# Two-level Strassen in the first MLP layer of the last two pairs

## The chip, the cores and the metric

The kernel runs on one core of one Trainium2 chip. Its engines each have their own instruction stream, in a fixed order: PE (TensorE: matmuls, with their weight loads shown as PEld), DVE (VectorE), ACT (ScalarE), POOL (GpSimd) and SP (SyncE, which here only issues DMAs). They wait for each other by semaphores. SBUF is the working memory of 128 partitions; PSUM, into which PE writes, has 8 banks of 512 fp32 per partition. The metric is the device time in microseconds, the median of several executions.

## The reference

```python
# attention: q, k, v [4, 8, 768, 64], blocks of 64 with a decaying state
for b in range(nb):
    intra = np.einsum('bhic,bhjc->bhij', qb, kb) * Dmask[None]
    intra = np.einsum('bhij,bhjd->bhid', intra, vb)
    inter = np.einsum('bhid,bhde->bhie', qb * lam_pow[None], kv_state)
    out[:, :, sl] = intra + inter
    kv_state = lam_block[None, :, None, None] * kv_state + np.einsum('bhsd,bhse->bhde', kb_dec, vb)
# then, with x [4, 768, 512] the heads side by side:
mixed = np.real(np.fft.fft(np.fft.fft(x, axis=1), axis=2))
u = x + mixed
un = (u - mu) / np.sqrt(var + 1e-06)          # over the last axis
ch = np.maximum(un @ w_ch1, 0.0) @ w_ch2      # 512 -> 2048 -> 512
out = u + ch
```

All of it is fp32. The change concerns `relu(un @ w_ch1)` for a third of the rows.

## The kernel before, in words

The 3072 rows are handled in 12 groups of 256 rows (two tiles of 128). The front (attention, Fourier mixing, normalisation) runs for all; the first four groups go through the MLP in the plain way while the fronts of later batches still run. The other eight groups, `LATE`, write their normalised rows transposed to DRAM (`utd`), and their rows `u` too (`ud`), and are done at the end, two groups at a time: four **pairs**, numbered 0 to 3, in `late(j)`. From about 439 us on there is only this work.

A pair computes both layers as one Strassen-Winograd product each: seven half-size products in place of eight, listed in `PRODUCTS` as (combination of weights or hidden rows, combination of the other operand). For the first layer the weights' combinations (`s2.A`) are made once; a pair's input combinations t1 to t4 are four sums on DVE (L737 to L740).

*First layer before.* For each of eight hidden chunks `i` of 128, the seven products are two accumulating matmuls of 128x128 by 256 columns each (`prod`, L773). Each fp32 matmul is two PE instructions, so this is 7*2*8*2 = 224 instructions per pair. ACT and DVE take the results out of PSUM in pieces of 256 elements per partition, apply the relu and form the sums that the second layer wants.

*Second layer.* It is Strassen a second time inside each of the seven products (`level2`): 49 quarter products of four 128x128 by 128 matmuls, so 49*4*2 = 392 instructions (L890). Within a product the seven quarter products come in groups 0 to 6 of eight PE instructions, and use three PSUM banks: X takes groups 0, 2, 4 and 6 one upon the other, Y group 1, Z groups 3 and 5. After each group the bank is read, by ACT where the target is fresh, else by an adding DVE operation:

```python
prod(X, S2, T2, False)
give(X, 1, 0, True)
```

As X goes on accumulating, group 2 can only be written when the read of group 0 is done, and so on. Two products are therefore interleaved by the loop at the end of `late`: product k gives its groups at the steps 7k, 7k+2, ..., 7k+12, so that in the steady state every step holds one group, and what follows a product is put down at step 7k+14. There are 8 bank buffers (`p2`), taken in turn.

The inner sums of the weights of the second layer (`td`) are made by POOL during pair 0's first layer (`keep_sums`: four sums per product, 28 in all, of 512 elements per partition), stored in DRAM, and loaded again by each pair, three tiles of 256 KB per product, into the six `tx` buffers. The inner sums of the hidden rows are made by DVE (`prepare_a`), in `sx` buffers, one product ahead. `split` replaces a quarter of an operand by a difference in place.

*Order.* Operations are recorded in the order of the Python code, and a scheduler of the framework then fixes an order per engine; what is pinned with `keep_in_program_order` stays. Each engine works strictly through its order, and an instruction whose semaphore is late holds all behind it. DMAs issued on SP's and ACT's queues (`nc.sync`, `nc.scalar`) wait in the same way. After product 4 of the second layer, DVE and POOL add the rows `u` (L843 on POOL, L870 on DVE) and the rows of the pair are stored (`store`: an SP DMA for one tile of each group, a POOL indirect DMA for the other).

Of the kernel before, what the change touches and what calls it, by code (L numbers as in the profile page):

```python
# [76 lines left out]
def kernel(  # L77
# [647 lines left out]

    def load_u(j, queue=nc.sync):

        r = s2.u[j] = new(s2.up, [128, 2, KO, G * 128], "ur")
        for h, (b, g) in enumerate(LATE[2 * j:2 * j + 2]):
            queue.dma_start(r[:, h], utd[b, g])  # L730


    def late(j):
        r = s2.u.pop(j)
        b11, b21, b12, b22 = r[:, 0, 0:2], r[:, 0, 2:4], r[:, 1, 0:2], r[:, 1, 2:4]
        t1, t2, t4 = (new(s2.hp, [128, 2, G * 128], "sx", bufs=7) for _ in range(3))
        V.tensor_tensor(t1, b12, b11, op=SUB)  # L737
        V.tensor_tensor(t2, b22, t1, op=SUB)  # L738
        V.tensor_tensor(t4, b21, t2, op=SUB)
        V.tensor_tensor(b12, b22, b12, op=SUB)  # L740
        U = dict(b11=b11, b21=b21, b22=b22, t1=t1, t2=t2, t4=t4, t3=b12)

        h = {n: new(s2.hp, [128, G, HF, 128], f"h{n}") for n in ("a11", "a12", "a22", "s1", "s3")}

        pre_a, pre_b = {}, {}

        def split(t):

            A11, _, A21, _ = quarters_a(t)
            tc.keep_in_program_order(V.tensor_tensor(A21, A11, A21, op=SUB))  # L750

        def prepare_a(k):

            a = PRODUCTS[k][0]
            A11, A12, A3, A22 = quarters_a(h[a])
            S1, S2, S4 = pre_a[k] = [new(s2.hp, [128, HF // 2, 128], "sx", bufs=7) for _ in range(3)]
            V.tensor_tensor(S2, A22, A3, op=SUB)
            yield 0.0
            V.tensor_tensor(S1, S2, A11, op=ADD)
            yield 0.0  # L760
            V.tensor_tensor(S4, A12, S2, op=SUB)
            yield 0.0

        def prepare_b(k):

            pre_b[k] = [new(s2.yp, [128, HF // 2, HM // 2], "tx", bufs=6) for _ in range(3)]
            for i in (1, 0, 2):
                nc.sync.dma_start(pre_b[k][i], s2.td[k][i])
                yield 0.0
# [9 lines left out]
        def bank():  # L779
            return new(s2.ps, [128, DM], "p2")[:, 0:G * 128]  # L780

        def finish(i, X, Z):
            a11, a12, a22, s1, s3 = (h[n][:, :, i, :] for n in ("a11", "a12", "a22", "s1", "s3"))
            prod(X, "s4", "b22", i, False)
            a21 = new(s2.hp, [128, G, 128], "a21", bufs=2)
# [7 lines left out]
        who = [[(b, TT[g][s]) for s in range(G)] for b, g in LATE[2 * j:2 * j + 2]]  # L793
        us = [new(s2.yp, [128, G, DM], "u2", bufs=2) for _ in range(2)]

        def load_x():
            for k in range(2):
                for s in range(G):
                    tc.keep_in_program_order(nc.sync.dma_start(us[k][:, s], ud[who[k][s]]))

        last = None
        for i in range(HF):
            a11, a12, a22 = (h[n][:, :, i, :] for n in ("a11", "a12", "a22"))
            X, Y, Z = bank(), bank(), bank()
# [15 lines left out]
            if j == 0 and i < len(PRODUCTS):  # L820
                if i == 0:
                    tc.keep_in_program_order(nc.gpsimd.tensor_copy(s2.begun, h["a11"][:, 0, 0, 0:1]))
                keep_sums(i)
            if i == HF - 3:
                load_x()
            if i == HF - 2:
                for k in range(2):
                    run(prepare_b(k))
            if i > HF // 2:
                split(h[("a11", "a12", "s3")[i - HF // 2 - 1]])  # L830
        run(prepare_a(0))
        finish(*last)
        run(prepare_a(1))
        if 2 * j + 2 < len(LATE):
            load_u(j + 1)

        yt = new(s2.yp, [128, 2, G, DM], "y2")
        T = new(s2.yp, [128, G, HM], "t2")
        y11, y12, y21, y22 = (yt[:, k, :, m:m + HM] for k in range(2) for m in (0, HM))

        def add_u(k, m, y):
            u = us[k][:, :, 0:HM] if m == 0 else us[k][:, :, DM - 1:HM - 1:-1]
            nc.gpsimd.tensor_tensor(y, y, u, op=ADD)  # L843

        def part_sum(o, x, y, op):

            for s in range(G):
                V.tensor_tensor(o[:, s], x[:, s], y[:, s], op=op)

        def after(k):  # L850

            if k == 0:
                h["s2"] = h["a11"]
                split(h["s1"])
                part_sum(h["a11"], h["s1"], h["a11"], SUB)
            elif k == 1:
                V.tensor_tensor(y11, y11, T, op=ADD)  # L857
                add_u(0, 0, y11)
            elif k == 2:
                split(h["a22"])  # L860
                h["s4"] = h["a12"]
                part_sum(h["a12"], h["a12"], h["s2"], SUB)
            elif k == 3:
                V.tensor_tensor(y21, T, y22, op=ADD)
                add_u(1, 0, y21)
            elif k == 4:
                V.tensor_tensor(y12, y12, T, op=ADD)
                V.tensor_tensor(y22, y22, y12, op=ADD)
                add_u(1, 1, y22)
                V.tensor_tensor(y12, y12, us[0][:, :, DM - 1:HM - 1:-1], op=ADD)  # L870
            elif k == 5:
                store(*who[1][1], yt[:, 1, 1])
            else:
                store(*who[0][1], yt[:, 0, 1])
                store(*who[1][0], yt[:, 1, 0])
                store(*who[0][0], yt[:, 0, 0])

        outs = [(T, True), (y11, True), (y22, True), (T, False), (y12, True), (y21, False), (y12, False)]

        def level2(k):  # L880

            (a, b), (y, fresh) = PRODUCTS[k], outs[k]
            A11, A12, A3, A22 = quarters_a(h[a])
            B11, T3, B21, B22 = quarters_b(s2.B[b])
            (S1, S2, S4), (T1, T2, T4) = pre_a.pop(k), pre_b.pop(k)
            X, Y, Z = (bank()[:, 0:HM // 2] for _ in range(3))

            def prod(ps, a, b, first):
                for i in range(HF // 2):
                    nc.tensor.matmul(ps, lhsT=a[:, i, :], rhs=b[:, i, :], start=(first and i == 0),  # L890
                                     stop=(i == HF // 2 - 1), skip_group_check=True)

            def give(ps, s, m, first=False):
                o = y[:, s, m * HM // 2:(m + 1) * HM // 2]
                if first and fresh:
                    nc.scalar.copy(o, ps)  # L896
                else:
                    V.tensor_tensor(o, ps, o, op=ADD)  # L898

            prod(X, A11, B11, True)  # L900
            give(X, 0, 0, True)
            yield 0.0
            prod(Y, A12, B21, True)
            give(Y, 0, 0)
            yield 0.0
            prod(X, S2, T2, False)
            give(X, 1, 0, True)
            yield 0.0
            prod(Z, A3, T3, True)
            give(Z, 1, 1, True)  # L910
            yield 0.0
            prod(X, S1, T1, False)
            give(X, 1, 1)
            yield 0.0
            prod(Z, A22, T4, False)
            give(Z, 1, 0)
            yield 0.0
# [101 lines left out]
    for j in range(len(LATE) // 2):  # L1019
        late(j)  # L1020
# [30 lines left out]
```

## Time and profile before

| | |
|---|---|
| median of 3 runs (lowest, highest) | 812.43 us (809.25, 812.84) |
| profiled execution, its own time | 816.68 us |
| its span, first to last instruction | 814.9 us |
| granted TensorE clock | 0.993 |
| PE busy | 780.8 us, 5280 instructions |
| DVE, ACT, POOL busy | 545.7, 203.6, 142.2 us |
| L773 on the chain, first layer of the pairs | 24% |
| L890 on the chain, second layer of the pairs | 19% |

A group of instructions in the profile is named by line, engine, operation, and output<-input by tile names, where `p` is a PSUM bank of the late stage, `ur` the loaded inputs, `w` and `w1s` the weights and their sums, `ha` and `hs` the hidden rows (a11, a12, a22; s1, s3), `sx` and `tx` the inner sums, `y` the output rows. Behind `x` stands the count, then busy time and the mean of one in ns, then the idle time ahead of them and what ended it. Matmuls overlap, so their mean (379 ns at L773, 275 at L890) is longer than their spacing, which the chain of work shows.

### The profile page before, as it was taken

The page shows a single profiled execution, that of the slowest core. Times are in us where ns is not written, and L with a number is a line of the kernel's source. Part 1 is how long each engine was busy: PE and PEld are TensorE (multiplying, and loading weights), DVE is VectorE, ACT ScalarE, POOL GpSimd, SP SyncE. Part 2 cuts the span into 40 slices and gives each one's busy share as a digit, 9 for nine tenths or more (in the row PEclk, how much of TensorE's full clock was granted, in tenths as well). Part 3 has the DMA queues.
Part 4 walks back from the last instruction along what each step waited for, and adds up shares of the span by engine and source line. Part 5 has one row for each costly group of instructions (what it writes and reads, how often), then busy time and mean ns, then how long its engine had stood idle before and what let it go on. Part 6 is the DMA issues. An engine that isn't in the chain of part 4 may idle for free.

```text
span 814.9 us, 13667 instructions
## 1 busy us (share of the span) xinstructions
PE 780.8 (96%) x5280; PEld 642.7 (79%) x5280; DVE 545.7 (67%) x1170; ACT 203.6 (25%) x512; POOL 142.2 (17%) x143
## 2 busy tenths in 40 slices
PE   6788999999999999999999999999999999999996
PEld 5667775858676766767846889988999889988996
DVE  6799979684853583246698997645865468735873
ACT  3464543314531211221201221022201221022210
POOL 3123223010101020121004950100011000100002
PEclk9899999999999999999999999999999999999999
DMA  9868643337853036442233374430346005440142
GB/s 222 229 149 217 172 136 104 103 63 191 215 139 100 26 78 138 107 129 101 52 65 104 142 251 150 131 117 1 104 126 193 7 1 156 130 142 0 40 130 78
DMA packets 141238, 96.54 MB, mean 118 GB/s; under 512 B 112766, under 2 KB 112766, under 8 KB 141174
## 3 DMA queue, kind: packets, MB, share of 16 engines
q1 hardware_dynamic: 136032, 83.20, 37.9%
q0 software_dynamic: 2112, 6.69, 2.4%
q10 hardware_dynamic: 3030, 5.78, 2.0%
q8 instruction: 42, 0.69, 0.4%
q14 instruction: 22, 0.18, 0.1%
HBM read 70.74 MB, written 24.91 MB: 117 GB/s over the span
## 4 chain that ended last, share of the span: by engine, by line
PE 75%; DVE 12%; DMA 6%; issue 4%; ACT 2%; POOL 1%; POOLq 0%; SPq 0%; ACTq 0%; DVEq 0%
PE p L773 24%; PE p L890 19%; PE pm L650 9%; PE pm L636 8%; PE pa L516 3%; PE pa L332 3%; PE pa L298 3%; DMA raw<-in_moe_w_ch_dram 3%; DMA x<-xb,ix 2%; PE pa L328 2%; PE pa L274 1%; PE pa L315 1%; PE pa L348 1%; DVE sc L302 1%; PE pa L279 1%
## 5 line engine op out<-in xcount | busy, mean ns | idle before, releaser
L636 PE MATMUL pm<-ut,w 128*128 128x256 f32 x512 | 119.2, 382 | 0.0
L650 PE MATMUL pm<-w,hr 128*128 128x512 f32 x256 | 115.8, 597 | 0.1
L636 PEld LDWEIGHTS pm<-ut,w 128*128 128x128 f32 x512 | 94.4, 190 | 15.4 <-issue 3.6
L773 PE MATMUL p<-ur,w 128*128 128x256 f32 x384 | 93.6, 379 | 0.1
L650 PEld LDWEIGHTS pm<-w,hr 128*128 128x128 f32 x256 | 46.6, 190 | 49.5 <-issue 48.0
L773 PEld LDWEIGHTS p<-ur,w 128*128 128x128 f32 x384 | 72.6, 190 | 10.6 <-issue 0.5
L843 POOL TENSOR_TENSOR y<-y,u 128x512 f32<-128x512 f32 x12 | 18.1, 1507 | 282.0 <-DVE y L857 214.0
L773 PE MATMUL p<-sx,w1s 128*128 128x256 f32 x256 | 65.8, 379 | 0.2 <-DVE sx L738 0.2
L890 PE MATMUL p<-tx,sx 128*128 128x128 f32 x448 | 59.5, 276 | 1.5 <-DVE y L898 1.5
L890 PEld LDWEIGHTS p<-tx,sx 128*128 128x128 f32 x448 | 54.5, 192 | 2.1 <-DVE y L898 2.1
L773 PEld LDWEIGHTS p<-sx,w1s 128*128 128x128 f32 x256 | 48.6, 190 | 7.2 <-issue 0.6
L898 DVE TENSOR_TENSOR y<-p,y 128x128 f32<-128x128 f32 x92 | 25.5, 287 | 31.0 <-PE p L890 23.0
L817 DVE TENSOR_TENSOR ha<-p,ha 128x256 f32<-128x256 f32 x32 | 13.5, 422 | 45.8 <-ACT ha L816 45.8
L270 POOL TENSOR_TENSOR kd<-k,decay 128x512 f32<-128x512 f32 x20 | 22.8, 1140 | 103.4 <-PE pa L315 55.0
L332 PE MATMUL pa<-sc,v 128*64 128x128 f32 x384 | 32.3, 287 | 7.7 <-DVE sc L302 7.7
L896 ACT COPY y<-p 128x128 f32<-128x128 f32 x48 | 12.8, 266 | 105.1 <-PE p L890 105.1
L302 DVE TENSOR_TENSOR sc<-pa,decay 128x512 f32<-128x512 f32 x48 | 31.5, 683 | 10.5 <-PE pa L298 10.4
L890 PE MATMUL p<-w,ha 128*128 128x128 f32 x288 | 37.4, 275 | 0.0
L298 PEld LDWEIGHTS pa<-qT,kT 64*128 64x128 f32 x384 | 25.9, 195 | 13.3 <-ACT qT L281 6.5
L332 PEld LDWEIGHTS pa<-sc,v 128*64 128x64 f32 x384 | 23.8, 140 | 15.4 <-DVE sc L302 9.6
L890 PEld LDWEIGHTS p<-w,ha 128*128 128x128 f32 x288 | 35.3, 192 | 0.4
L298 PE MATMUL pa<-qT,kT 64*128 64x128 f32 x384 | 30.6, 294 | 3.3 <-ACT qT L281 2.4
(172 smaller groups left out, 1431.7 us busy)
## 6 DMA issues: line engine op xcount, KB each, us to landing
tx<-td SPq DMA_DIRECT2D x84, 256.0 KB
raw<-in_moe_w_ch_dram SPq DMA_DIRECT2D x32, 512.0 KB
k<-in_k_dram SPq DMA_DIRECT2D x24, 256.0 KB
q<-in_q_dram SPq DMA_DIRECT2D x24, 256.0 KB
v<-in_v_dram SPq DMA_DIRECT2D x24, 256.0 KB
td<-tx SPq DMA_DIRECT2D x21, 256.0 KB
ud<-x SPq DMA_DIRECT2D x16, 256.0 KB
utd<-e SPq DMA_DIRECT2D x64, 64.0 KB
```

What stands on the lines that cost most here:

```text
L270: nc.gpsimd.tensor_tensor(kd, kt, kpow, op=ALU.mult)
L298: mm(pss[hi][:, hp, :], lhsT=kT[HD[hi], hp, :], rhs=qT[HD[hi], hp, :], start=True, stop=True)
L302: nc.vector.tensor_tensor(t, pss[hi], decay[:, hi::2, :], op=ALU.mult)
L328: mm(po[HD[hi], hp, :], lhsT=s_old[HD[hi], hp, :], rhs=qs[HD[hi], hp, :], start=(hp == 0), stop=False, skip_group_check=True)
L332: mm(po[HD[hi], hp, :], lhsT=vt[:, 2 * hp + hi, :], rhs=sc[hi][:, hp, :], start=(c == 0 and hp == 0), stop=(hp == HP - 1), skip_group_chec ...
L516: mm = nc.tensor.matmul(ps[0:m, n, :], lhsT=piece(a, i, n), rhs=cs[0:rows, a, i in (2, 3), n, :], start=(a == 0), stop=(a == 1))
L636: nc.tensor.matmul(ps, lhsT=w1[:, c, 128 * fc:128 * fc + 128], rhs=ut[:, c, :], start=(c == 0), stop=(c == KO - 1))
L650: nc.tensor.matmul(ps, lhsT=hr[(fc - f0) // 4][:, fc % 4, 128 * i:128 * i + 128], rhs=w2[:, fc, :], start=(fc == f0), stop=(fc == f1 - 1))
L773: nc.tensor.matmul(ps, lhsT=s2.A[a][:, kt, 128 * i:128 * i + 128], rhs=U[b][:, kt, :], start=(first and kt == 0), stop=(kt == 1), skip_gro ...
L843: nc.gpsimd.tensor_tensor(y, y, u, op=ADD)
L890: nc.tensor.matmul(ps, lhsT=a[:, i, :], rhs=b[:, i, :], start=(first and i == 0), stop=(i == HF // 2 - 1), skip_group_check=True)
L898: V.tensor_tensor(o, ps, o, op=ADD)
```

## The change

Pairs 2 and 3 (from `DEEP = 2` on) compute the first layer with the second level of Strassen as well; pairs 0 and 1 stay as they are. Each of the seven products becomes seven quarter products of 128 deep by 512 hidden by 128 rows: four matmuls of 128 columns, into the four quarters of a bank (`deep_first`). The bank is read as a whole, 512 elements per partition, and added into one of the hidden tiles; the outer sums and the relus follow when a product is complete, on POOL (`part_sum(nc.gpsimd, ...)`), DVE and ACT. The inner sums of the inputs are made in `inputs`, partly on POOL. The inner sums of the weights are made by POOL beside pair 1's first layer (`keep_sums_w`, four per product, stored to `sd`); the fourth, a difference, is put back in the weights' place by seven DMAs on ACT's queue (`place_sums_w`) once pair 1's first layer has read them. The second layer of pair 1 and all 28 products of pairs 2 and 3 then run in one interleaved stream (`in_step`), where before each pair's second layer was a stream of its own. `sx` has six buffers instead of seven, and `sv` replaces `a21` with three.

In the code of L-numbers of the changed kernel: L739 is `keep_sums_w`'s sum, L745 the placing DMA, L760 a load of sums, L847 `split`, L861 to L865 `prepare_a`, L939 `part_sum`, L964 the new matmuls, L971 and L973 their reads by ACT and DVE, L976 and L982 relus, L1072 `sum_s3`, L1023 to L1031 the second layer.

```diff
+    def keep_sums_w(k):
+        A11, A12, A21, A22 = quarters_w(s2.A[PRODUCTS[k][0]])
+        S3, S2, S1, S4 = [new(s2.yp, [128, FH // 2], "tx", bufs=6) for _ in range(4)]
...
+        for i, o, x, y, op in ((3, S3, A11, A21, SUB), (1, S2, A22, S3, SUB), (0, S1, S2, A11, ADD), (2, S4, A12, S2, SUB)):
+            pin(nc.gpsimd.tensor_tensor(o, x, y, op=op))
+            nc.sync.dma_start(s2.sd[k][i], o)
+    def place_sums_w():
+        for k, (a, _) in enumerate(PRODUCTS):
+            nc.scalar.dma_start(quarters_w(s2.A[a])[2], s2.sd[k][3])
+    def inputs(j):
...
+        B11, B12, B21, B22 = (r[:, :, k::2, m:m + 128] for k in range(2) for m in (0, 128))
+        V.tensor_tensor(B12, B22, B12, op=SUB)
+        t1 = U["t1"] = sx([128, 2, G * 128])
+        V.tensor_tensor(t1, b12, b11, op=SUB)
+        V.tensor_tensor(b12, b22, b12, op=SUB)
+        T2, T1, T4 = [sx([128, 2, 2, 128]) for _ in range(3)]
+        V.tensor_tensor(T2, B12, B11, op=ADD)
+        V.tensor_tensor(T1, B22, T2, op=SUB)
+        V.tensor_tensor(T4, B21, T2, op=SUB)
...
+        V.tensor_tensor(t2, b22, t1, op=SUB)
+        V.tensor_tensor(t4, b21, t2, op=SUB)
+        for i, n in enumerate(("t2", "t1", "t4")):
+            nc.gpsimd.tensor_tensor(q2[:, i], C12, C11, op=ADD)
+            nc.gpsimd.tensor_tensor(q1[:, i], C22, q2[:, i], op=SUB)
+            nc.gpsimd.tensor_tensor(q4[:, i], C21, q2[:, i], op=SUB)
-        t1, t2, t4 = (new(s2.hp, [128, 2, G * 128], "sx", bufs=7) for _ in range(3))
+    def part_sum(e, o, x, y, op):
+        for s in range(G):
+            e.tensor_tensor(o[:, s], x[:, s], y[:, s], op=op)
+    def seven(mm, read, first=()):
+        X, Y, Z = (bank() for _ in range(3))
+        for m, ps, start, where in ((0, X, True, (0, 0, 1)), (1, Y, True, (0, 0, 0)), (2, X, False, (1, 0, 1)),
+                                    (3, Z, True, (1, 1, 1)), (4, X, False, (1, 1, 0)), (5, Z, False, (1, 0, 0)),
+                                    (6, X, False, (0, 1, 1))):
+            mm(m, ps, start)
+            read(ps, *where)
+            yield 0.0
+    def deep_first(j, k):
...
+        y, fresh = (("s1", 1), ("a11", 1), ("a22", 1), ("s1", 0), ("s3", 1), ("a12", 0), ("s3", 0))[k]
...
+        def mm(m, ps, start):
+            for i in range(HF // 2):
+                nc.tensor.matmul(ps[:, 128 * i:128 * i + 128], lhsT=ab[m][0][:, 128 * i:128 * i + 128], rhs=ab[m][1],
+                                 start=(start and i == 0), stop=True, skip_group_check=True)
+        def read(ps, r, s, first):
+            o = h[y][:, s, HF // 2 * r:HF // 2 * (r + 1)]
+            if first and fresh:
+                nc.scalar.copy(o, p)
+            else:
+                V.tensor_tensor(o, p, o, op=ADD)
+            done[r, s] = done.get((r, s), 0) + 1
+            if k > 4 and done[r, s] == (1 if (r, s) == (0, 1) else 2):
+                nc.scalar.activation(o, o, AF.Relu)
+        yield from seven(mm, read)
...
+        T, a11, a12, a21, a22 = (h[n] for n in ("s1", "a11", "a12", "s3", "a22"))
+        if k == 1:
+            part_sum(nc.gpsimd, a11, a11, T, ADD)
+            relu(a11)
+        elif k == 3:
+            part_sum(nc.gpsimd, a12, T, a22, ADD)
+        elif k == 4:
+            part_sum(nc.gpsimd, a21, a21, T, ADD)
+            part_sum(V, a22, a22, a21, ADD)
+            relu(a22)
+            load_x(j)
+            open_y(j)
+            split(a11)
+            run(prepare_a(j, 0))
+        elif k == 5:
+            split(a22)
+            split(a12)
+        elif k == 6:
+            split(a21)
+            part_sum(V, T, a21, a22, ADD)
+            if j + 1 < PAIRS:
+                load_u(j + 1)
+    def sum_s3(j):
+        for s in range(G):
+            V.tensor_tensor(h["s3"][:, s], h["a11"][:, s], h["s3"][:, s], op=SUB)
-            if j == 0 and i < len(PRODUCTS):
+            if j < min(DEEP, 2) and i < len(PRODUCTS):
-                keep_sums(i)
+                (keep_sums, keep_sums_w)[j](i)
+    def late():
+        for j in range(PAIRS):
+            if j < DEEP:
+                open_pair(j)
+                if j == 0:
+                    run(inputs(0))
+                first_layer(j)
+                if j + 1 < DEEP:
+                    in_step(second_layer(j) + [(inputs(j + 1), iter(()))])
+        place_sums_w()
+        in_step(second_layer(DEEP - 1) + [w for j in range(DEEP, PAIRS) for w in deep_pair(j)])
-    for j in range(len(LATE) // 2):
-        late(j)
+    late()
```

In the new stream the products of a pair are numbered 0 to 6 in the first layer and go on with 0 to 6 of the second; a step of the stream that holds one group of eight PE instructions is what the prediction calls a slot, and slot 0 is the first group of the pair's first product, so that the second layer's product k begins at slot 49+7k.

## The prediction

> **What bounds the kernel now.** I read the head of the page first, then the waits of TensorE (PE) in the late stage (439 us to the end), the chain, the table by stage, the timeline and the groups.
>
> ```profile
> span 814.9 us, 13667 instructions
> PE 780.8 (96%) x5280; PEld 642.7 (79%) x5280; DVE 545.7 (67%) x1170; ACT 203.6 (25%) x512; POOL 142.2 (17%) x143
> ...
> PE p L890 <- DVE y L898: 1.5, 3, 0.5
> PE p L773 <- DVE sx L738: 0.2, 1, 0.2
> ```
>
> PE waits 1.7 us in the whole late stage, 0.5 us at each of three pair boundaries. What is saved there is PE's own work, and any wait put in is lost at once. The chain gives the rates:
>
> ```profile
> 530.57 46.62 PE p L773 x216
> 577.19 0.67 PE p L890 x6
> 577.86 1.79 PE p L773 x8
> 579.65 32.40 PE p L890 x290
> ```
>
> A first-layer instruction (256 columns) takes 46.62/216 = 0.2158 us, a second-layer one (128 columns) 32.40/290 = 0.1117; a group of eight takes 0.894 us. I call that a slot. The next question is how free the helpers are:
>
> ```profile
> 455.00:463.00 8.00, 8.00 (x39) 6.95 (x38) 7.83 (x13) 2.04 (x6) 7.84 (x7) 1.00 0.44 164
> ...
> 551.00:559.00 8.00, 8.00 (x39) 7.04 (x38) 3.29 (x10) 1.87 (x5) 0.00 (x0) 1.00 0.00 0
> ```
>
> Columns: width, busy PE, weight load, VectorE (DVE), ACT, POOL. The first row is pair 0 with GpSimd's (POOL's) sums beside it, the second pair 1 without. The same DVE work fills 7.83 of 8 us in one and 3.29 in the other, and the timeline shows why:
>
> ```profile
> 458.45 0.41 DVE L790 TENSOR_TENSOR hs<-a,ha 128x256 f32<-128x256 f32 x1
> 458.79 1.49 DVE L791 TENSOR_TENSOR hs<-ha,a 128x256 f32<-128x256 f32 x1
> 460.20 0.41 DVE L788 TENSOR_TENSOR ha<-p,ha 128x256 f32<-128x256 f32 x1
> ...
> 458.46 1.54 POOL L723 TENSOR_TENSOR tx<-w2s 128x512 f32<-128x512 f32 x1
> ```
>
> L791, two SBUF inputs, started while a POOL sum ran, and ended 0.28 us after that sum's end (460.00). L788, which reads PSUM, kept its 0.41 beside the next sum. Prices:
>
> ```profile
> L302 DVE TENSOR_TENSOR sc<-pa,decay 128x512 f32<-128x512 f32 x48 | 31.5, 683 | 10.5 <-PE pa L298 10.4
> L276 ACT COPY kT<-pa 128x512 f32<-128x512 f32 x24 | 14.1, 588 | 26.0 <-PE pa L274 26.0
> L757 DVE TENSOR_TENSOR sx<-ha 128x512 f32<-128x512 f32 x20 | 13.8, 690 | 2.8 <-PE p L890 2.4
> L848 DVE TENSOR_TENSOR ha<-ha,ha 128x1024 f32<-128x1024 f32 x8 | 9.7, 1216 | 0.0
> L270 POOL TENSOR_TENSOR kd<-k,decay 128x512 f32<-128x512 f32 x20 | 22.8, 1140 | 103.4 <-PE pa L315 55.0 <-DMA k<-in_k_dram 31.1 <-issue 14.0
> ```
>
> By the timeline, back-to-back DVE operations start 0.60 us apart at 512 elements (two L302 take 1.29) and 1.13 at 1024; two ACT copies start 0.48 apart; DVE starts a read 0.20 us after its group's last issue; PE resumes 0.25 after the read it waited for (524.70 to 524.95).
>
> [...] A POOL sum of 512 with DVE idle took 1.26 us here (at 441.06)[...]. Bounds: 1.95 (512 took 1.06 and 256 took 0.62 at 341 us, where one operand is broadcast) and 2.7 (twice the 1.35 mean of L723). [...]
>
> **The change, part by part.** *Removed:* pairs 2 and 3 lose 224 instructions of 0.2158 (48.34 us) and get 49 groups of eight at 0.1117 (392, 43.79 us). Gain 4.55 us a pair, 9.1 us in all. I take the old second-layer rate because shapes and weight loads are the same; if it were half of a first-layer instruction (0.1079), 1.5 us a pair more would be saved, which I don't count on.
>
> *Pair 1's sums:* 28 POOL sums of about 1.35 us, 38 us beside 48 us of PE. Pair 0 has as many, with PE at 8.00 of 8: free, as long as DVE's lag stays inside the bank rotation. Their 28 stores (SP issues, 0.33 us each) replace none; 7 copies back go on ACT's queue among the last column's PSUM copies, 0.33 us each (L730's issue). Two stand directly ahead of a copy that frees X: 0.3 and 0.5 us, 0.8 in sum, bounds 0 and 3 (their semaphores are shared with transfers just issued, and the DMA share is 0.88 at this place in pair 0; 1.75 MB are added).
>
> *Loads of sums:* three of 256 KB per product, as the second layer has now; a slot is refilled 11 to 13 slots (10 us) ahead. Free; without that cover each costs a transfer of 2 to 3 us. SP also has the output stores standing between them, as today.
>
> *Boundaries:* eight input sums on DVE instead of four, spread between reads of 0.2 us, and nine small POOL sums, done by about slot 8 and wanted at slot 25. The 0.5 us stays.
>
> *DVE in a deep first layer:* 33 reads at 0.60, 8 input, 4 split and 6 prepared sums at 0.60, six of 1024 at 1.13: 37.4 us of 43.8. It fits, so its order decides. I walked three places, slot n starting 0.894n after the pair's first group. A bank must be read before the group that writes it next.
>
> 1. Slot 17 (product 1, group 5) ends at 16.09, DVE reads it to 16.98, POOL adds T to a11's first half 17.08 to 19.43. ACT has the relu of this half queued ahead of two PSUM copies: relu to 20.43, copies to 20.91 and 21.50. Slot 24 rewrites the second one's bank: 21.75 against 21.46 due. **0.3 us.**
> 2. Slot 38 (product 4, group 5) is read by 35.76 (later by place 1, as is everything here). POOL adds T to a21: 35.86 to 38.21 and 38.21 to 40.56. DVE's next in order is L939, a22 += a21. Its semaphore comes at 38.3, when POOL is in its second half, so it is held like L791: done about 41.6. Behind it stand the read of slot 41 (to 42.3), the second L939 (42.2 to 43.4), a split (44.0) and the read of slot 42 (to 44.65). Slot 46 rewrites that bank: 44.9 against 41.12. **3.8 us.** DVE is then late twice more, for slots 47 and 50 (preparing sums stand between): **0.3 each.**
> 3. The copy for slot 56, which ends at E, stands ahead of the last two relus on ACT (done E+1.0). From E+1.1 DVE does T=a21+a22, a split, s3=a11-a21, three preparing sums, s2 (each 1024-wide sum in two halves) and short reads, in all six at 1.13, four at 0.60 and three at 0.20: 9.8 us. The read of slot 64 ends at E+11.2; slot 68 is due at E+9.83 and can start at 11.45. **1.6 us.**
>
> Sum per pair 0.3+3.8+0.6+1.6 = 6.3, less 4.55: +1.75. Two pairs +3.5, pair 1 +0.8: +4.3. Against the profiled execution: span 814.9 to 819.2 (816.68 to 821.0 with what lies around it). That execution is 4.25 above the median of 812.43, so the forecast is 812.43+4.3 = **816.7 us**. The tail after PE is unchanged. Bounds of the POOL sum (1.95 and 2.7) move a pair by -1.1 and +1.0 us: 814.5 to 818.7; with the ACT issues, 813.5 to 821.
>
> **The rivals.** *DVE's lateness doesn't reach PE at product 4* (the other side): if place 2 were covered by the banks, 1.9 us a pair stay: -9.1+3.8+0.8 = -4.5, 807.9. It decides below 2.1 us of waits per pair. For it: in pair 0 DVE ran full and PE stayed at 8.00. Against: there no bank was rewritten by the same product, here X is, four slots later.
>
> *Waits and gain cancel:* POOL's sum at 1.95 and no hold of L939: place 1 nothing, place 2 39.76+0.1+1.13+0.6+0.69+0.25-41.12 = 1.4 and 0.6, place 3 1.6: 3.6 a pair, -9.1+7.2+0.8 = -1.1, 811.3. Against: L791's 1.49.
>
> *DVE becomes the bound:* if POOL's sums hold eight more of DVE's two-input sums by 1.2 us each, 37.4 becomes 47.0, 3.2 a pair above the slots: 816.7+6.4 = 823. For it: 7.83 of 8. Against: most reads are from PSUM. A late load of a sum would look alike in time.
>
> **How the numbers follow.** Forecast 0.44, covered 0.13, cancel 0.25, DVE bound 0.18. A measurement tells about 0.5% (4.1 us) from no change, so the forecast lies at the border: of its 0.44, 0.30 is slower and 0.14 the same. Faster 0.13 and 0.02 of "cancel": 0.15; same 0.14+0.23 = 0.37; slower 0.30+0.18 = 0.48. The forecast's own range is 813.5 to 821; the whole one, 807 to 824, leaves half of "covered" and a third of "DVE bound" outside.
>
> **What would show it.** PE busy on the 128-column first layer near 43.8 us a pair; waits of PE for VectorE of 4 to 5 us in each of pairs 2 and 3 at products 5 and 6, with L939 of about 3 us behind a POOL sum; one of 1 to 2 us some twelve slots into the second layer; 0.3 for an ACT copy behind a relu. Wrong if PE's waits there stay under 2 us, if the new groups take other than 0.894 us, or if waits name DMA.

## The result, and the profile after

| | before | after |
|---|---|---|
| median (lowest, highest) of 22 executions each | 809.96 us (808.13, 815.26) | 817.28 us (810.14, 821.82) |
| the same, in a later session (44 and 6 executions) | 809.93 us (807.12, 814.04) | 816.22 us (812.96, 820.78) |
| profiled executions: time, mean granted TensorE clock | 816.68 us, 0.993 | 810.14 us, 0.997; later session 817.06 us, 0.991 |

The ratio is 1.0080 with a 95% interval of 1.0062 to 1.0098, and 1.0084 (1.0056 to 1.0113) in the later session: slower by 0.8%, 6.3 to 7.3 us. The forecast was 816.7 us, which is 4.3 us over the median of three, 812.43, that it started from. The two medians of 810 are 2.5 us under that start, so the measured difference is 2 to 3 us larger than the forecast one, and the time was met as closely as it was only because the start was too high by about as much.

The first profile of after happens to be the fastest of its 22 executions, so I use a second one as well, of the later session; it lies near that session's median. The head of the first profile:

```profile
span 808.4 us, 14556 instructions
PE 770.1 (95%) x5616; PEld 642.5 (79%) x5616; DVE 580.9 (72%) x1126; ACT 215.5 (27%) x504; POOL 216.3 (27%) x202
```

PE has 336 instructions more and 10.7 us less of busy time than before. Up to 5.1 us of that is the low clock in the front of before's profile (10.24 us at half clock); the rest is the new first layer, which does save. Who PE waited for in the late stage (430 us to the end; us in total, times, longest), first profile of after:

```profile
PE p L964 <- DVE ha L973: 3.9, 2, 1.9
PE p L964 <- DVE hs L973: 2.2, 2, 1.1
PE p L882 <- ACT ha L904: 1.6, 1, 1.6
PE p L1023 <- DVE y L1031: 1.3, 3, 0.5
PE p L882 <- DVE sx L786: 0.2, 1, 0.2
```

9.2 us, where there were 1.7. The first two lines are product 4 of the deep pairs, one wait of 1.94 and one of 1.11 us in each of pairs 2 and 3. The timeline of after shows that place (start, duration):

```profile
649.92 4.66 POOL L939 TENSOR_TENSOR hs<-hs,hs 128x1024 f32<-128x1024 f32 x2 [1.58 <-DVE hs L973]
...
652.31 3.35 DVE L939 TENSOR_TENSOR ha<-ha,hs 128x1024 f32<-128x1024 f32 x1 [1.57 <-POOL hs L939]
...
655.59 0.68 DVE L973 TENSOR_TENSOR ha<-p,ha 128x512 f32<-128x512 f32 x1
...
656.19 1.21 DVE L939 TENSOR_TENSOR ha<-ha,hs 128x1024 f32<-128x1024 f32 x1
656.41 1.13 PE L964 MATMUL p<-sv,w 128*128 128x128 f32 x8 [1.94 <-DVE ha L973]
...
657.92 0.68 DVE L973 TENSOR_TENSOR hs<-p,hs 128x512 f32<-128x512 f32 x1
...
658.66 1.16 PE L964 MATMUL p<-sx,tx 128*128 128x128 f32 x8 [1.11 <-DVE hs L973]
```

It is place 2 of the forecast: DVE's a22 += a21 starts when POOL's first half is done, runs beside POOL's second half and takes 3.35 us instead of the 1.21 of the next one; the two bank reads behind it come late, and PE waits for each.

From the first matmul of the late stage to PE's last, before took 371.94 us (436.69 to 808.63) and this after 372.35 (428.19 to 800.54), both with the clock at 1.00 there. **So the fastest execution of after is level with before, and the waits alone don't make 6 or 7 us.** The second profile of after has a late stage of 377.22 us, 4.9 us more, with nearly the same waits (9.9 us in sum; the one for ACT is 0.9 longer). The other 4 us stand in its table of stretches, at the same place of pair 2 (columns: stretch, width, busy PE, PEld, DVE, ACT, POOL; then the granted clock, DMA share and GB/s):

```profile
656.00:658.00 2.00, 1.15 (x11) 0.95 (x9) 2.00 (x1) 0.00 (x0) 1.25 (x1) 1.00 0.98 320
658.00:660.00 2.00, 0.92 (x8) 0.95 (x8) 2.00 (x4) 1.06 (x1) 0.00 (x0) 1.00 0.85 304
660.00:662.00 2.00, 0.89 (x5) 0.70 (x5) 2.00 (x5) 1.06 (x1) 0.00 (x0) 0.86 0.04 16
662.00:664.00 2.00, 2.00 (x12) 2.00 (x11) 2.00 (x4) 0.63 (x1) 0.00 (x0) 0.50 0.00 0
664.00:666.00 2.00, 2.00 (x16) 2.00 (x16) 2.00 (x5) 1.17 (x2) 0.00 (x0) 0.78 0.48 131
666.00:668.00 2.00, 2.00 (x21) 2.00 (x20) 1.60 (x4) 0.80 (x2) 0.00 (x0) 1.00 0.46 131
```

The pauses end at 659.08 and 661.33. Then, from 661.46 to 664.87, PE runs at half clock: 12 and 16 instructions in 2 us where 20 or 21 are usual. (1 - clock) times width, 1.71 us are lost. In pair 3 the low stretch is twice as long, 753.62 to 760.45, 3.41 us lost by the same sum; a part of it falls into the second pause, which ends at 755.11, and costs nothing there. From boundary to boundary (the end of PE's wait of 0.4 to 0.5 us for DVE at the turn of two pairs) pair 2 takes 93.78 us in place of the first profile's 92.24, and pair 3 with the end of PE's work 99.59 in place of 97.14: 4.0 us for the clock. With the 0.9 of the longer wait for ACT that is the 4.9. The forecast has nothing of this kind.

Two theories go into the experiments. **Pauses and clock:** the made waits cost their length, and on top of it the granted clock falls to a half behind some of them. **Rivals:** the clock falls for another reason (the denser work of 128 columns, GpSimd's extra sums, the transfers at that place), or it is chance and falls in the front as often, as in the profile of before (0.5 to 0.65 at 28 to 36 and 76 to 80 us).

### The profile page after: what moved, and what is told of

Same layout as the page of the kernel before. It is cut to its first block, busy times and chain, and to the rows that moved or that the text cites. A ratio compares the mean times of both kernels' runs of the same rounds, so it can differ in the third digit from the quotient of the medians.

```text
span 808.4 us, 14556 instructions
## 1 busy us (share of the span) xinstructions
PE 770.1 (95%) x5616; PEld 642.5 (79%) x5616; DVE 580.9 (72%) x1126; ACT 215.5 (27%) x504; POOL 216.3 (27%) x202
## 4 chain that ended last, share of the span: by engine, by line
PE 71%; DVE 13%; DMA 7%; issue 4%; ACT 2%; POOL 2%; POOLq 0%; ACTq 0%; SPq 0%; DVEq 0%
PE p L1023 19%; PE p L882 12%; PE p L964 9%; PE pm L650 8%; PE pm L636 8%; DMA raw<-in_moe_w_ch_dram 3%; PE pa L516 3%; PE pa L332 3%; PE pa L298 3%; DMA x<-xb,ix 2%; PE pa L328 2%; DVE ha L939 1%; PE pa L274 1%; PE pa L315 1%; PE pa L279 1%
## 5 line engine op out<-in xcount | busy, mean ns | idle before, releaser
L1023 PE MATMUL p<-tx,sx 128*128 128x128 f32 x416 | 55.3, 276 | 1.3 <-DVE y L1031 1.3
L1023 PEld LDWEIGHTS p<-tx,sx 128*128 128x128 f32 x416 | 50.6, 192 | 1.9 <-DVE y L1031 1.9
L882 PE MATMUL p<-ur,w 128*128 128x256 f32 x192 | 46.9, 379 | 0.1
L882 PEld LDWEIGHTS p<-ur,w 128*128 128x128 f32 x192 | 36.3, 190 | 5.7 <-issue 0.5
L973 DVE TENSOR_TENSOR hs<-p,hs 128x512 f32<-128x512 f32 x40 | 27.4, 689 | 18.6 <-PE p L964 17.9
L1031 DVE TENSOR_TENSOR y<-p,y 128x128 f32<-128x128 f32 x92 | 25.5, 287 | 18.8 <-PE p L1023 12.6
L1023 PE MATMUL p<-w,ha 128*128 128x128 f32 x288 | 37.7, 275 | 0.0
L550 POOL TENSOR_SCALAR ve<-mv 128x2 f32<-128x2 f32 x12 | 3.4, 285 | 123.0 <-DVE mv L547 123.0
L1023 PEld LDWEIGHTS p<-w,ha 128*128 128x128 f32 x288 | 35.2, 192 | 0.2
L882 PE MATMUL p<-sx,w1s 128*128 128x256 f32 x128 | 33.1, 381 | 1.8 <-ACT ha L904 1.6
L644 ACT ACTIVATE hr<-pm 128x256 f32<-128x256 f32 x44 | 16.7, 385 | 67.4 <-PE pm L636 67.0
```

Source lines behind the costliest of these rows:

```text
L882: nc.tensor.matmul(ps, lhsT=s2.A[a][:, kt, 128 * i:128 * i + 128], rhs=U[b][:, kt, :], start=(first and kt == 0), stop=(kt == 1), skip_gro ...
L973: V.tensor_tensor(o, p, o, op=ADD)
L1023: nc.tensor.matmul(ps[:, 0:HM // 2], lhsT=ab[m][0][i], rhs=ab[m][1][:, i, :], start=(start and i == 0), stop=(i == HF // 2 - 1), skip_grou ...
L1031: V.tensor_tensor(o, ps[:, 0:HM // 2], o, op=ADD)
```

## The experiments

All medians below are of the session that the experiment ran in; before has 809.93, 809.73 and 809.38 us in the three sessions.

### The changed kernel once more

> The changed kernel itself, once more. In the two profiles so far the late stage is level (364.85 us before, 365.25 after, both with the clock at 1.00 there), and the waits of TensorE there rose from 1.7 to 9.2 us while its work fell by 9. So the measured 0.8% must lie in something that the profiled execution, the fastest of 22, doesn't have. Clock theory: this run's executions again spread over 810 to 822 us with mean granted clock 0.985 to 0.997, a profile at about 0.99 shows windows under 1.00, and these lie in the late stage (from 430 us on), where the change is; waits of PE there stay near 9 us. Rival, chance: the windows under 1.00 lie in the front, as in the profile of before (20 to 80 us), and the kernel before loses as much in its own runs; then the 0.8% is no property of the late stage. Rival, waits: a profile at 817 us shows more than 13 us of waits of PE from 430 us on.

816.22 us; the profile and its stretches are those just shown. The expectation counts the late stages from 7.1 us later on; their difference of 0.4 is the same. All stretches under 1.00 that lie in the work of this profile are at the place-2 pauses, none in the front. The chance rival falls for this execution; the waits rival too (9.9 us, not 13).

### The sums a21 += T on VectorE

```diff
-            part_sum(nc.gpsimd, a21, a21, T, ADD)
+            part_sum(V, a21, a21, T, ADD)
```

> In the changed kernel the two sums a21 += T go to VectorE instead of GpSimd, so that no GpSimd sum runs beside a22 += a21. By the walk of place 2: reads up to slot 38 done at 35.8 us, two sums of 1.13, then two more of 1.13, a split and a read: about 40.9 against the bank's due time of 41.1, so the wait of 3.05 us a pair (1.94 and 1.11 in the profile) falls to 0.3 to 1.2. Two pairs: 4 to 5.5 us less than the changed kernel, about 812 beside its 817, about even with the kernel before. If place 2 isn't what costs time, it stays within 2 us of the changed kernel. If the granted clock is the larger part, the mean clock stays at 0.99 or so and the kernel stays slower than before by 2 to 3 us.

**804.95 us, 0.9950 of before (0.9933 to 0.9967): faster than both kernels**, by 5.0 and by 11.3 us. About 812 was expected, from the length of the waits alone: 11.3 us is nearly twice the 5.9 that the second profile of after lists at place 2. The timeline at this place and the table of stretches of this kernel:

```profile
651.84 1.23 DVE L939 TENSOR_TENSOR hs<-hs,hs 128x1024 f32<-128x1024 f32 x1
...
653.58 1.22 DVE L939 TENSOR_TENSOR hs<-hs,hs 128x1024 f32<-128x1024 f32 x1
...
655.31 2.35 DVE L939 TENSOR_TENSOR ha<-ha,hs 128x1024 f32<-128x1024 f32 x2
```

```profile
654.00:656.00 2.00, 2.00 (x20) 2.00 (x20) 2.00 (x3) 0.00 (x0) 0.00 (x0) 1.00 0.80 234
656.00:658.00 2.00, 2.00 (x20) 2.00 (x20) 2.00 (x3) 1.30 (x2) 0.00 (x0) 1.00 0.98 351
658.00:660.00 2.00, 2.00 (x19) 2.00 (x19) 2.00 (x5) 1.08 (x2) 0.00 (x0) 1.00 0.58 222
```

DVE does four sums of 1.2 us where it was held for 3.35, reads lie between them, and PE has no wait at place 2 at all. DVE is full here, the DMAs are as busy as at this place in after (0.98), PE does the same 128-column work, and the clock stays at 1.00 through the whole late stage: none of the three takes the clock. The late stage is 366.26 us. Against the first profile of after, at full clock, the two deep pairs are 3.6 us each shorter (88.64 in place of 92.24, 93.53 in place of 97.14). That is what place 2 costs: its two waits are listed with 3.05 us because the list counts from the modelled end of the last matmul, while PE's groups start 2.10 and 1.35 us late. Against the second profile they are 5.1 and 6.1 us shorter: twice 3.6 for the waits and 4.0 for the clock. The edit takes away both the wait for GpSimd's first half (1.57 us) and the hold by its second; it doesn't tell the two apart.

### GpSimd's sums alone, and one deep pair alone

```diff
-    DEEP = 2
+    DEEP = 4
...
-        place_sums_w()
```

> The changed kernel with no deep pair: GpSimd still makes and stores the weights' sums beside pair 1 (28 sums, 28 stores), but nothing copies the fourth back and pairs 2 and 3 run the first layer with 256-column instructions as before. If GpSimd's sums beside pair 1 cost nothing, as forecast, this is the kernel before within 1 us, also in the granted clock. If the extra work of GpSimd and the stores lowers the clock or holds VectorE, it is 2 us or more slower than before.

810.43 us, 1.0017 (1.0007 to 1.0028). PE's waits in the late stage:

```profile
PE p L1023 <- DVE y L1031: 1.2, 3, 0.4
PE p L882 <- DVE sx L786: 0.2, 1, 0.2
```

Pair 1 with POOL's 28 sums takes 92.84 us from boundary to boundary (516.48 to 609.32), as against 92.93 before. So the sums and their stores are hidden in this profile, at full clock from 13 us on. The median is 0.5 us over before with an interval just clear of 1, and the median of its executions' mean clocks is 0.997 where before has 0.998; where that half microsecond comes from was not traced.

```diff
-    DEEP = 2
+    DEEP = 3
```

> Only the last pair has the deep first layer; pairs 0 to 2 run it with 256-column instructions. Waits theory: gain 4.55, waits 3.05 at product 4 and 1.6 at the ACT copy: level with the kernel before within 1.5 us at equal clock. Clock theory (the denser 128-column first layer lowers the granted clock): about half of the changed kernel's loss, 3 to 4 us slower than before, mean clock between the two. If the loss comes with GpSimd's sums beside pair 1 and not with the deep pairs, it is as slow as the changed kernel or slower.

811.05 us, 1.0011 (0.9997 to 1.0026): neither the 3 to 4 us of the clock theory's dose nor a clear nothing. Its profile has one pair of pauses at place 2 (1.94 and 0.39 us) and, in the late stage, one fall of the clock, 751.60 to 755.01, just behind the first; the late stage is 371.54, as before. So pair 3's gain, its wait and its 1.71 us nearly cancel. The executions' median mean clock, 0.995, lies between before's 0.998 and after's 0.990. The wait for ACT isn't there at all: the seven copies back are issued when pair 2's first layer is done, a whole pair after the sums were stored.

### The copies back on other queues

```diff
-            nc.scalar.dma_start(quarters_w(s2.A[a])[2], s2.sd[k][3])
+            nc.sync.dma_start(quarters_w(s2.A[a])[2], s2.sd[k][3])
```

and in the other kernel

```diff
-            nc.scalar.dma_start(quarters_w(s2.A[a])[2], s2.sd[k][3])
+            nc.gpsimd.dma_start(quarters_w(s2.A[a])[2], s2.sd[k][3])
```

Both start from the version with the a21 sums on VectorE. What they should remove, in the second profile of after (ACTq is a DMA issue on ACT's queue):

```profile
569.51 0.33 ACTq L745 DMA_DIRECT2D w<-sd  x1
569.88 0.37 ACT L904 COPY ha<-p 128x256 f32<-128x256 f32 x1 [5.12 <-DMA tx<-td]
...
570.30 1.13 PE L882 MATMUL p<-sx,w1s 128*128 128x256 f32 x4 [2.50 <-ACT ha L904]
```

The first copy back waits for a transfer of the second layer's sums that SP had just issued; ACT's bank copy stands behind it, and PE loses 2.50 us.

> The version with the two a21 += T sums on VectorE, and the seven copies back of the weights' sums issued by SyncE instead of ScalarE. ScalarE then copies its banks of pair 1's last column in time, and TensorE's wait of 2.2 us for it (1.6 and 2.5 us in the two profiles of the changed kernel) should be gone: 802 to 803.5 us, faster than before by 0.9% (ratio 0.989 to 0.993). If the copies now hold SyncE's queue and later loads come late, a wait of TensorE for a DMA shows and the time is 805 or more.

> The version with the a21 sums on VectorE, and the seven copies back of the weights' sums issued by GpSimd, behind its last sum of pair 1, instead of by ScalarE. Neither ScalarE's bank copies nor SyncE's loads stand behind them then. TensorE's wait of 2.2 us for ScalarE at pair 1's last column should go and no new one come: 802 to 803.5 us, ratio to before about 0.991. If GpSimd's issues hold VectorE's sums[...] or come late, 804.95 or more.

806.76 us with SyncE, 0.9951 (0.9933 to 0.9969), and 807.11 with GpSimd, 0.9963 (0.9946 to 0.9980): no gain over 804.95, where 802 to 803.5 was expected of both. Nor is a loss shown: in the profile with GpSimd's issues the late stage is 365.30 us, 1.0 less than with ACT's, and it starts 2.8 us later, behind a front that the edit doesn't touch. The wait for ACT is gone, and a new one has come, of 1.79 us there and of 2.21 with SyncE, where the clock falls behind it (584.04 to 587.46). In the kernel with GpSimd's issues, the waits of PE and the timeline of DVE:

```profile
PE p L1023 <- DVE t L1031: 1.8, 1, 1.8
```

```profile
582.94 0.69 DVE L796 TENSOR_TENSOR ur<-ur 128x512 f32<-128x512 f32 x1 [3.29 <-DMA ur<-utd]
```

The first input sum of pair 2 waits for pair 2's rows, and a bank read stands behind it. In the version with ACT's issues the same sum runs at 583.74 without waiting. Two things moved against it: the scheduler put L796 four sums earlier in DVE's order, and the rows land 8.7 us after their issue instead of 4.4 (6.4 with SyncE), at 582.92. By these times neither alone would have made a wait (an estimate): in the old order DVE would have come to L796 at about 583.1, and with the old 4.4 us the rows would have been there at 578.7, before its turn at 579.6. No run separates them.

### Pauses made on purpose

A pause of PE was built into the version with the a21 sums on VectorE, with nothing else changed. In the first attempt the pause was a rewrite of one column of weights by itself:

```diff
+            if k in (1, 3, 5) and m == 2:
...
+                for _ in range(n):                       # n = 1, 4, 8
+                    nc.scalar.copy(sc, ps[:, 0:HM // 2])
+                t = ab[3][1][:, 0, 0:1]
+                nc.scalar.copy(t, t)
```

> The version with the a21 sums on VectorE, with nine made pauses of TensorE in the second layer of pairs 1 to 3: after the third group of products 1, 3 and 5 ScalarE copies that group's bank to a spare tile once, and then rewrites one column of the next group's weights with itself; the next group waits for that. About 0.8 us each, 7 us in all by their length: 812. If a pause costs its length alone, time minus 804.95 is the sum of the pauses in the profile, and the clock stays at 0.997. If even short pauses lower the granted clock, some windows behind them show under 1.00 and the time is 3 us or more above that sum.

> As with the short pauses, with four copies in each: about 1.6 to 2.2 us a pause, as long as the first wait at product 4 of the changed kernel; by length alone 15 to 20 us, 820 to 825. Clock theory: after some of the nine pauses the windows show the clock at 0.5 for 2 to 8 us, each costing 1 to 4 us more, so that the time is 5 us or more above base plus pauses and the mean clock falls under 0.99. Rival (the clock fell in the changed kernel for its transfers or its VectorE load at that place, not for the pause): clock at 0.997, time equal to base plus pauses.

> As before, with eight copies in each: 2.7 to 3.5 us a pause, 25 to 31 us by length. Clock theory: nearly every pause is followed by windows at 0.5, 2 us or more lost for each: 15 us or more above base plus pauses, mean clock 0.97 or lower. Rival: time equal to base plus pauses.

826.17, 826.10 and 829.34 us, nearly the same for all three: they don't test the length. Nothing tied the rewrite to the group before it, the scheduler moved it ahead into pair 0's first layer, and there ACT waited for POOL's sums of these same weights. PE's waits in the kernel with one copy:

```profile
PE p L882 <- ACT ha L914: 7.5, 1, 7.5
PE p L882 <- ACT ha L911: 6.8, 2, 4.2
```

All three profiles show the clock at 0.5 within this wait of 7.5 us and for 5.1 to 5.9 us behind it (mean granted clock 0.982, 0.986 and 0.985, where the version without pauses has 0.998), which speaks for the theory, for long pauses only.

In the second attempt ACT multiplies the group's bank by zero into a tile and adds a zero of that tile to the column, so that the order follows from the data:

```diff
+            if k in (1, 3, 5) and m == 2:
+                z = new(s2.yp, [128, HM // 2], "zz")
+                for _ in range(n):                       # n = 3, 6, 10
+                    nc.scalar.activation(z, ps[:, 0:HM // 2], AF.Copy, scale=0.0)
+                t = ab[3][1][:, 0, 0:1]
+                nc.scalar.activation(t, t, AF.Identity, bias=z[:, 0:1])
```

> The pauses once more, now tied by data so that they stand where they were meant: in the version with the a21 sums on VectorE, behind the third group of products 1, 3 and 5 of the second layer of pairs 1 to 3 ScalarE multiplies that group's bank by zero into a spare tile three times and adds a zero of it to one column of the next group's weights, for which TensorE waits; nine pauses. Here 0.5 to 1.2 us each. Pause alone: 804.95 plus the waits in the profile, clock 0.997. Clock theory: below some length a pause triggers nothing; I expect none or few windows at 0.5 here, and the time within 3 us of base plus waits.

> The same with six operations, pauses of 1.5 to 2.3 us, as long as the first wait at product 4 of the changed kernel. Clock theory: behind a part of the nine pauses the clock goes to 0.5 for 3 to 8 us, each costing 1.5 to 4 us; the time is 5 us or more above base plus waits. Rival (the clock fell in the changed kernel for its transfers or its VectorE load at that place): clock at 0.997 and the time within 3 us of base plus waits.

> The same with ten operations, pauses of 2.7 to 3.6 us. Clock theory: behind most of the nine the clock goes to 0.5, 15 us or more above base plus waits. Rival: base plus waits.

The expectations count nine pauses; pair 0's second layer goes through the same code, so there are twelve, of up to 0.95, of 1.20 to 1.88 and of 2.44 to 2.73 us. The medians are 814.62, 824.80 and 851.90. Late stages against the 366.26 and the 4.1 us of waits of the base, each from its profile:

| | late stage over base | waits over base | half clock | left |
|---|---|---|---|---|
| up to 0.95 us | 7.6 | 3.9 | 0 | 3.7 |
| 1.20 to 1.88 us | 19.9 | 16.2 | 1 x 1.71 | 2.0 |
| 2.44 to 2.73 us | 46.8 | 28.7 | 10 x 1.71 | 1.0 |

What is left is 0.1 to 0.3 us a pause; why it isn't the same for all three stays open. The table of stretches at the same pause of pair 0 (the one ahead of product 3's fourth group), first in the kernel with the long pauses, then with the middle ones:

```profile
504.00:506.00 2.00, 0.04 (x1) 0.04 (x1) 0.29 (x1) 1.68 (x6) 0.00 (x0) 0.98 0.35 118
506.00:508.00 2.00, 2.00 (x9) 2.00 (x10) 0.00 (x0) 0.00 (x0) 0.00 (x0) 0.50 0.00 0
508.00:510.00 2.00, 2.00 (x14) 2.00 (x13) 1.58 (x3) 0.27 (x1) 0.00 (x0) 0.67 0.00 0
```

```profile
502.00:504.00 2.00, 0.67 (x6) 0.67 (x7) 0.29 (x1) 1.15 (x5) 0.00 (x0) 1.00 0.48 174
504.00:506.00 2.00, 2.00 (x20) 2.00 (x19) 1.44 (x3) 0.27 (x1) 0.00 (x0) 1.00 0.00 0
```

Here DVE and POOL have next to nothing to do, the DMAs are busy for a third of the stretch, and PE does its ordinary second layer: the pause alone takes the clock, and a longer one takes it more often. All pauses of PE from 0.7 us on in the late stages of nine profiles (both of after, one deep pair, a21 sums on VectorE, the two with other queues, the three of the second attempt), and how many were followed by half clock within 9 us:

| pause | followed by half clock |
|---|---|
| up to 1.60 us | 0 of 17 |
| 1.79 to 1.94 us, with at most 0.4 behind it | 2 of 4 |
| 2.19 to 2.50 us | 3 of 7 |
| 2.67 to 2.73 us | 8 of 8 |
| place 2 of after: 1.94 and 0.88 to 1.11 us with 1.1 us of work between | 2 of 4 |

Each fall takes 1.71 us, once twice that.

What decides between two pauses of the same length can be read from the same traces. Within each of the 14 profiles all changes of the granted clock lie on one grid of 3.413 us: in the second profile of after, from 661.46 to 753.62 it is 27.0 of these, and in the profile of before, from 35.44 to 76.40, 12.0. PE's busy time in such windows at place 2 of pair 2, first in the first profile of after, then in the second:

```profile
652.81:656.22 3.41, 1.67 (x15) 1.48 (x14) 3.41 (x3) 0.52 (x1) 1.77 (x1) 1.00 0.99 344
656.22:659.63 3.41, 2.10 (x16) 1.94 (x17) 3.41 (x6) 1.59 (x2) 0.00 (x0) 1.00 0.26 100
```

```profile
654.63:658.05 3.42, 2.52 (x23) 2.32 (x21) 3.07 (x1) 0.00 (x0) 2.62 (x2) 1.00 0.90 297
658.05:661.46 3.41, 1.26 (x9) 1.10 (x10) 3.41 (x6) 2.11 (x2) 0.00 (x0) 1.00 0.51 184
661.46:664.87 3.41, 3.41 (x17) 3.41 (x18) 3.41 (x7) 1.13 (x2) 0.00 (x0) 0.50 0.13 21
```

The same two pauses are cut by the grid into windows with 49% and 62% of busy PE in one execution, and the clock stays; into 74% and 37% in the other (the second window holds 1.03 us of the first pause and the whole of the second), and the next window runs at half. Over the late stages of all 14 profiles, those of the first attempt included, of the windows at full clock with at most 42% of busy PE 20 of 20 were followed by one at half clock, of those with 43 to 45% 3 of 4, and of the 1481 with 48% or more none. (In the front, 3 of 10 windows with 48 to 55% were followed by one too.) Windows at half clock with up to 74% of busy PE were followed by another one, as in pair 3 of the second profile; those with 88% or more were not. So in these late stages 1.9 us or more of idle PE inside one window (at most 45% busy) took the clock for the next in 23 of 24 cases, and 1.8 us or less (48% and more) in none. The eight pauses of 2.67 to 2.73 us are no eight draws: the two of a pair lie 17.1 us apart, which is five windows, and so meet the grid at the same place. By these shares (an estimate) a pause of that length that the grid cuts in half would pass.

## Why the prediction came out as it did

The time was forecast within a tenth of a per cent and the sign was right, but the sum is made of other terms than the forecast's, and its start of 812.43 was 2.5 us high: that it was met so closely is luck.

**PE's work.** Forecast 4.55 us a deep pair. Pair 2 from boundary to boundary took 92.94 us before and 88.64 with the a21 sums on VectorE, which has the same PE work and no wait inside: 4.3. Over the whole late stage (366.26 - 371.94, less 2.4 us by which the waits rose) the work is 8.0 us shorter where 9.1 was forecast; about 0.45 of the difference is in pair 1, whose period outside its waits rose by that much.

**Place 2: mechanism and size right.** L939 was to be held from 38.3 to 41.6; in the first profile of after slot 0 starts at 613.94, and L939 runs from 38.4 to 41.7, 3.35 us, behind POOL sums of 2.33 each. The walk's 2.35 for such a sum was the author's estimate: no trace of before shows one of 1024 elements, only the bounds of 1.95 and 2.7 are worked out from it. The hold that before shows at 256 elements (L791 took 0.42 us each time in pair 1, and 1.48 to 1.49 in six of its eight times in pair 0, beside POOL's sums) is there for these larger sums as well, 3.35 against 1.21. Slot 46, forecast at 44.9, starts at 44.7 in both deep pairs. Its delay came in two parts, because slot 45 rewrites the bank whose read stands directly behind L939; the forecast's 3.8 us held both. Measured it is 3.6, by the periods of the pairs. The twice 0.3 us after it did not come: PE's order is not that of the slots there, as at place 3.

**Places 1 and 3 cost nothing.** At place 1 everything stands as walked, and PE's group starts at 635.45 without a wait of its own in the list (the view is the timeline of after):

```profile
630.99 2.35 POOL L939 TENSOR_TENSOR ha<-ha,hs 128x1024 f32<-128x1024 f32 x1 [9.32 <-DVE ha L973]
...
633.38 1.06 ACT L982 ACTIVATE ha<-ha 128x1024 f32<-128x1024 f32 x1 [1.68 <-POOL ha L939]
...
634.34 1.06 ACT L971 COPY ha<-p 128x512 f32<-128x512 f32 x2
```

The forecast's 0.3 is at most 0.1. (The relu took 1.06 us; the walk has 1.0, the author's estimate, for which before shows no relu of 1024 elements.) At place 3 the step that failed is the assumption that PE takes its groups in the order of the slots:

```profile
669.70 1.23 DVE L939 TENSOR_TENSOR hs<-hs,ha 128x1024 f32<-128x1024 f32 x1 [0.70 <-ACT hs L976]
...
677.25 2.36 DVE L939 TENSOR_TENSOR ha<-hs,ha 128x1024 f32<-128x1024 f32 x2
...
678.62 1.06 PE L1023 MATMUL p<-w,hs 128*128 128x128 f32 x8
...
679.51 0.61 PE L1023 MATMUL p<-w2s,ha 128*128 128x128 f32 x4
679.52 0.29 DVE L1031 TENSOR_TENSOR y<-p,y 128x128 f32<-128x128 f32 x1
...
679.96 1.06 PE L1023 MATMUL p<-w,sx 128*128 128x128 f32 x8
```

DVE did what was walked. Slot 56 ends at E = 668.67; the chain lasts from 669.70 to 679.61, 9.9 us where 9.8 were forecast, and the read of slot 64 ends behind it at 679.81, E+11.1 where E+11.2 was forecast. Slot 68 (the last group of product 1, the one that takes an inner sum from `sx` with a quarter in `w`) starts at E+11.3, forecast at E+11.45. But PE doesn't idle till then: the scheduler has put slot 69 (`w,hs`) and half of slot 70 (`w2s,ha`) ahead of it, 1.34 us of work in place of the 1.6 us of waiting. In the same way two instructions of slot 48 stand ahead of slot 47, and six of slot 51 ahead of slot 50.

**The copies back.** POOL's sums and their stores were free, as forecast. The 0.8 us for the copies was worked out from issue times; what counted was the wait of the first issue for a transfer, 1.6 and 2.5 us in the two profiles, which the forecast had named only as the reason for its upper bound of 3.

**What was not priced: the clock.** At full clock, in the first profile, the change comes out even: each deep pair gains 4.3 us and loses 3.6 at place 2, -1.4 for the two; pair 1 takes 94.81 us in place of 92.93, +1.9. The sum is +0.5, and the whole late stage measured +0.4. The forecast had +3.5 and +0.8 for these two. The 6 to 7 us that were measured come in the main from the clock that the place-2 pauses take, 4.0 us in the second profile, beside 0.9 of a longer wait for ACT. Mean clock over after's 22 executions goes from 0.997 to 0.985 and their times from 810.14 to 821.82. The median clock, about 0.990, is 0.007 under that of the fastest; at 3.41 us of half clock in some 812 us, 0.0021 each, that is three to four falls, at most 5 to 7 us. The number 816.7 was met because waits that were not there (3.2 us at place 3, 1.2 behind place 2) and a high start stood in for a cost that was not seen.

**The rivals.** "DVE's lateness doesn't reach PE" was wrong, but its world exists: with that lateness taken away the kernel is 5.0 us faster than before, where this rival said 4.5, though with 3.8 us of waits at the other places that did not come. "Waits and gain cancel" was right about the waits of the fastest execution and wrong about the hold of L939. DVE did not become the bound.

## What to carry to other kernels

Price a pause of TensorE not at its length alone: from about 1.8 us on, here, add a chance of 1.71 us of half clock, so that two waits of together 3 us cost 3.6 at full clock and 5 to 6 where the clock fell. What counted here was the idle time inside one window of 3.41 us, so two waits close together can count as one: 1.94 and 0.88 to 1.11 us with 1.1 us of work between took the clock in 2 of 4 cases. The two-input GpSimd sum that still ran beside a two-input VectorE sum held the latter (3.35 us in place of 1.21, done 1.08 us behind GpSimd's end), and all bank reads behind it with it; the same sums on the busier VectorE were 11 us better. A wait that follows from a walk through slots is one only if the engine's order has no other ready work in between: read the order from the trace. Where a profile is the fastest of its executions, look at a typical one before explaining a median by it.

## What was not expected of the hardware

In these profiles the clock fell in a fixed unit: one stretch of 3.41 us at 0.5, 1.71 us lost, in 14 of the 15 falls behind pauses of the table above, and two such stretches in the fifteenth. All its changes lie on a grid of the same 3.41 us in each profile, and a window of that grid need not be idle throughout. In the late stages it was enough, in 23 of 24 cases, that PE was busy for at most 45% of it, 1.9 us or more of idle, so that pauses of 1.88 to 2.73 us took the clock, and two of 1.94 and 0.88 to 1.11 with 1.1 us of work between them in 2 of 4 cases. That the outcome of one and the same pause differs from execution to execution is where it lies on the grid, as the two profiles of after show: windows with 49% and 62% of busy PE in one, with 74% and 37% in the other.
